# Sliding-window attention and a squared-ReLU FFN: first four chunks ahead of the weights, casting weight loads, an order written by hand, and crossbar transposes in the later blocks

## The chip, the cores and the metric

One core of a Trainium2 chip. The metric is the device time of one execution, in microseconds; the median of several runs counts. Engines are written PE (TensorE; PEld is its weight load), DVE (VectorE), ACT (ScalarE), POOL (GpSimd) and SP (SyncE, which issues transfers).

## What is computed

```python
# q, k, v: (8, 8, 576, 64) float32; moe_w_in: (512, 2048); moe_w_out: (2048, 512)
scores = (1/sqrt(D)) * q @ k.T          # per batch and head
mask = (rel >= 0) & (rel < 64)          # rel = query position - key position
attn = softmax(where(mask, scores, -1e9))
x = (attn @ v).transpose(0, 2, 1, 3).reshape(4608, 512)
h = maximum(x @ w_in, 0)
out = (h * h) @ w_out                   # (4608, 512) float32
```

## The kernel before

The 4608 tokens are cut into 36 chunks of 128 tokens and into 9 blocks of four chunks (512 tokens). Each query block of 64 tokens needs at most the 64 keys before it and its own 64. All matmuls are in float16.

For a chunk, `load` brings k, q and v as three tiles of 128 tokens x 8 heads x 64 (262 KB each, rows of 256 bytes) by SP's queue, and POOL casts them to float16 (L160 to L167). v is kept twice, in tiles shifted by 64 tokens (`v_ev`, `v_od`). Then four steps follow:

- `transposes` (L169): eight PE transposes bring k and q to head-dimension-major form in PSUM; DVE copies k to `kT` (L180), which also carries the 64 keys of the chunk before (L177), and ACT copies q to `qT` (L182).
- `scores` (L185): sixteen small matmuls, Exp on ACT (L199), and a minimum with a mask on DVE (L201).
- `values` (L204): sixteen small matmuls with a column of ones for the sum, then reciprocal and product on DVE (L215, L216), which give `x_sb`.
- `to_xT` (L221): four PE transposes of x and a DVE copy to `xT` (L226), one tile per block.

`ffn_up` takes a block: for each of 16 slices of d_ff, four matmuls of 512 columns (L250), a ReLU on ACT (L254) and a product on DVE (L255), which gives the square of the ReLU in `h2`. `ffn_up_chunk` does the same for one chunk, four slices at a time (L271 to L276), and is used for blocks 0 and 1. `ffn_out` does, for each 128 tokens of a block, 16 matmuls of 512 columns (L296), a copy by ACT that undoes the scale of the weights (L301) and an output transfer on SP (L303).

The weights come as float32 pieces of 262 KB through the pool `wst`: 16 of w_in, scaled by 100 and cast on DVE (L117), and 16 of w_out, cast on POOL (L130).

The program first asks for chunk 0, then all of w_in, then chunks 1 to 6, with `warm` matmuls between the steps of chunk 0; then chunk 7, w_out, and the ups of chunks 0 to 7 with the attention of the next chunks woven in. After that, the loop over g takes the output of block g-1, the up of block g, the attention of block g+1 and the loads of block g+2, mixed by `weave`. The framework's scheduler decides the final order on each engine: in the trace single matmuls of one group can stand between those of another.

Of the kernel before, what the change touches and what calls it, by code (L numbers as in the profile page):

```python
# [9 lines left out]
FP32 = mybir.dt.float32  # L10
# [3 lines left out]


def weave(*streams):

    keyed = []
    for s, (steps, lo, hi) in enumerate(streams):
        n = len(steps)  # L20
        for i, step in enumerate(steps):
            keyed.append((lo + (hi - lo) * (i + 0.5) / n, s, i, step))
    keyed.sort(key=lambda e: e[:3])
    return [e[3] for e in keyed]
# [3 lines left out]
def kernel(  # L28
# [17 lines left out]
    W_SCALE = 100.0  # L46
    OUT_SCALE = 1.0 / (W_SCALE * W_SCALE)
# [6 lines left out]
    wst = ctx.enter_context(tc.tile_pool(name="wst", bufs=4))  # L54
    stage = ctx.enter_context(tc.tile_pool(name="stage", bufs=15))
    st16 = ctx.enter_context(tc.tile_pool(name="st16", bufs=8))
    attw = ctx.enter_context(tc.tile_pool(name="attw", bufs=3))
# [8 lines left out]

    ident = const.tile([P, P], FP16, name="ident")
    make_identity(nc, ident[:])

    base = const.tile([P, 64], FP16, name="base")
    nc.gpsimd.memset(base[:], BIG)
    nc.gpsimd.affine_select(
        out=base[:], in_=base[:], compare_op=ALU.is_ge, fill=0.0, base=-1,
        pattern=[[-1, 64]], channel_multiplier=1,
    )
    nc.gpsimd.affine_select(  # L80
        out=base[:], in_=base[:], compare_op=ALU.is_ge, fill=0.0, base=64,
        pattern=[[1, 64]], channel_multiplier=-1,
    )
# [10 lines left out]
    mask_first = make_mask("mask_first", 0)  # L94
    mask_inner = make_mask("mask_inner", None)
    mask_second = make_mask("mask_second", 1)

    w_in_sb = const.tile([P, DMC, DFF], FP16, name="w_in_sb")
    w_out_sb = const.tile([P, FFC, DM], FP16, name="w_out_sb")

    NV = 8
    v_evs = [const.tile([P, H, 66], FP16, name=f"v_ev{i}") for i in range(NV)]
    v_ods = [const.tile([P, H, 66], FP16, name=f"v_od{i}") for i in range(NV)]
    for i in range(NV):
        nc.vector.memset(v_evs[i][:, :, 64:65], 1.0)
        nc.vector.memset(v_ods[i][:, :, 64:65], 1.0)
    nc.vector.memset(v_ods[0][0:64, :, 0:D], 0.0)

    def load_w_in():
        steps = []  # L110
        FQ = DFF // 4

        def one(quar, c):
            ws = wst.tile([P, FQ], FP32, name="ws", tag="ws")
            nc.sync.dma_start(out=ws[:], in_=moe_w_in[c * P:(c + 1) * P,  # L115
                                                      quar * FQ:(quar + 1) * FQ])
            nc.vector.tensor_scalar(  # L117
                out=w_in_sb[:, c, quar * FQ:(quar + 1) * FQ], in0=ws[:],
                scalar1=W_SCALE, scalar2=None, op0=ALU.mult)

        for quar in range(4):
            for c in range(DMC):
                steps.append(lambda quar=quar, c=c: one(quar, c))
        return steps

    def load_w_out():
        def one(f):
            ws = wst.tile([P, DM], FP32, name="ws2", tag="ws")
            nc.sync.dma_start(out=ws[:], in_=moe_w_out[f * P:(f + 1) * P, :])
            nc.gpsimd.tensor_copy(out=w_out_sb[:, f, :], in_=ws[:])  # L130

        return [lambda f=f: one(f) for f in range(FFC)]


    xTs = {}

    def xT_of(g):
        if g not in xTs:
            xTs[g] = xtp.tile([P, DMC, 512], FP16, name="xT", tag="xT")
        return xTs[g]  # L140

    q16s, k16s, qTs, kTs, pms, xs = {}, {}, {}, {}, {}, {}

    def load(i):

        sts = []
        for (src, nm) in ((k, "k"), (q, "q"), (v, "v")):
            st = stage.tile([P, H, D], FP32, name=f"{nm}_st", tag="st")
            b0, j0 = divmod(2 * i, NB)
            if j0 + 1 < NB:  # L150
                nc.sync.dma_start(  # L151
                    out=st[:], in_=src[b0, :, 64 * j0:64 * j0 + P, :].rearrange("h p d -> p h d"))
            else:
                nc.sync.dma_start(
                    out=st[0:64], in_=src[b0, :, 64 * j0:S, :].rearrange("h p d -> p h d"))
                nc.sync.dma_start(
                    out=st[64:P], in_=src[b0 + 1, :, 0:64, :].rearrange("h p d -> p h d"))
            sts.append(st)
        k16s[i] = st16.tile([P, H * D], FP16, name="k16", tag="k16")
        nc.gpsimd.tensor_copy(out=k16s[i][:], in_=sts[0][:].rearrange("p h d -> p (h d)"))  # L160
        q16s[i] = st16.tile([P, H * D], FP16, name="q16", tag="q16")
        nc.gpsimd.tensor_copy(out=q16s[i][:], in_=sts[1][:].rearrange("p h d -> p (h d)"))
        v_ev, v_od, v_next = v_evs[i % NV], v_ods[i % NV], v_ods[(i + 1) % NV]
        nc.gpsimd.tensor_copy(out=v_ev[:, :, 0:D], in_=sts[2][:])
        nc.gpsimd.tensor_copy(out=v_od[64:P, :, 0:D], in_=v_ev[0:64, :, 0:D])
        if i + 1 < NCK:
            nc.gpsimd.tensor_copy(out=v_next[0:64, :, 0:D], in_=v_ev[64:P, :, 0:D])  # L167
# [201 lines left out]
```

The softmax here doesn't subtract the row's maximum and nothing guards it: scores larger than these inputs give would overflow.

## Time and profile before

| | |
|---|---|
| median of 3 runs | 347.73 us (347.43 to 350.61) |
| span of the profiled execution, its own time | 345.9 us |
| PE busy | 324.3 us (94%), 3146 matmuls |
| DVE, ACT, POOL busy | 207.9, 163.8, 121.5 us |
| read from HBM, written | 36.70 MB, 9.44 MB |
| k, q, v tile of 262 KB | 3.9 to 4.1 us from issue to landing |
| output tile of 262 KB | 2.2 us from issue to landing |

The median of the runs is 1.8 us above the profiled span. In the profile, the busy rows cut the span in 40 slices of 8.6 us and give the busy share of each in tenths; a row of a timeline has its start, its duration, the engine, the line and the tiles. Matmuls overlap in the records, so what one costs is read from the distance of starts, not from its duration.

### The profile page before, as it was taken

To read this page: it belongs to the slowest core of one execution; us is meant where nothing else is said; L and a number is where in the kernel's file an instruction comes from. 1 tells how busy PE (TensorE), PEld (TensorE's weight loads), DVE (VectorE), ACT (ScalarE), POOL (GpSimd) and SP (SyncE) were. 2 spreads that over 40 slices of the span, in tenths; PEclk is the share of its full clock that TensorE was granted. 3 is DMA by queue.
4 is the path that set the end of the run, shared out by engine and by line. 5 is a ranking of instruction groups with operands and counts; after the bars stand their busy time and mean duration, and the time that the engine had idled before them with its cause. 6 is when DMAs were issued, how large, how long until landed. Compare 5 with 4: busy or idle time off the path is not lost.

```text
span 345.9 us, 7917 instructions
## 1 busy us (share of the span) xinstructions
PE 324.3 (94%) x3146; PEld 178.2 (52%) x3146; DVE 207.9 (60%) x506; ACT 163.8 (47%) x289; POOL 121.5 (35%) x204
## 2 busy tenths in 40 slices
PE   1957888999999999999999999999999999999995
PEld 0346787875555555445545554455445544544442
DVE  2656988852666776676776657665675566544400
ACT  1123457544535646643664466436544654444411
POOL 4009895497753333316566544530000000000000
PEclk9996999999999999999999999999999999999998
DMA  7799987899972455546877757730011000000021
GB/s 200 249 252 239 234 247 252 207 230 228 243 172 61 93 121 123 121 124 155 212 185 182 170 135 184 185 87 27 23 45 36 30 32 32 30 30 32 35 88 62
DMA packets 122341, 46.65 MB, mean 135 GB/s; under 512 B 113600, under 2 KB 113600, under 8 KB 122304
## 3 DMA queue, kind: packets, MB, share of 16 engines
q1 hardware_dynamic: 122304, 46.15, 51.7%
q8 instruction: 24, 0.39, 0.5%
q14 instruction: 13, 0.11, 0.1%
HBM read 36.70 MB, written 9.44 MB: 133 GB/s over the span
## 4 chain that ended last, share of the span: by engine, by line
PE 83%; DVE 7%; DMA 5%; ACT 2%; SPq 1%; issue 1%; ACTq 0%
PE ops L296 37%; PE hps L250 28%; DMA ws<-in_moe_w_in_dram 5%; PE qkT_ps L173 4%; PE av L211 4%; PE xt_ps L224 2%; DVE h_397 L276 1%; DVE h_1087 L276 1%; DVE xT L226 1%; DVE w_in_sb L117 1%; PE hps_639 L271 1%; SPq L151 1%; SPq L115 0%; PE hps_1088 L271 0%; PE hps_1537 L271 0%
## 5 line engine op out<-in xcount | busy, mean ns | idle before, releaser
L250 PE MATMUL hps<-xT,w_in_sb 128*128 128x512 f16 x448 | 115.2, 379 | 0.0
L254 ACT ACTIVATE hrelu<-hps 128x512 f32<-128x512 f32 x112 | 66.8, 598 | 91.6 <-PE hps L250 90.9
L250 PEld LDWEIGHTS <-w_in_sb 128*128 128x128 f16 x448 | 43.7, 98 | 52.6 <-issue 0.3
L271 PEld LDWEIGHTS <-w_in_sb 128*128 128x128 f16 x512 | 31.2, 99 | 8.2 <-issue 3.9
L301 ACT ACTIVATE osb<-ops 128x512 f32<-128x512 f32 x36 | 21.6, 600 | 29.1 <-PE ops L296 28.9
L182 ACT ACTIVATE qT<-qkT_ps 128x512 f16<-128x512 f16 x36 | 21.5, 596 | 22.6 <-DVE kT L180 22.3
L216 DVE TENSOR_TENSOR x_sb<-av,rden 128x256 f16<-128x256 f32 x72 | 27.5, 415 | 0.1
L180 DVE COPY kT<-qkT_ps 128x512 f16<-128x512 f16 x36 | 15.2, 421 | 18.0 <-PE qkT_ps L173 17.8
L226 DVE COPY xT<-xt_ps 128x512 f16<-128x512 f16 x36 | 15.1, 420 | 12.7 <-PE xt_ps L224 12.7
L215 DVE RECIPROCAL rden<-av 128x4 f32<-128x4 f32 x72 | 11.4, 178 | 17.1 <-PE av L211 17.1
L255 DVE SCALAR_TENSOR_TENSOR h_5222<-hps,hrelu 128x512 f16<-128x512 f32 x16 | 11.1, 691 | 16.6 <-ACT hrelu L254 16.6
L296 PE MATMUL ops<-w_out_sb,h_1087 128*128 128x512 f16 x64 | 17.5, 380 | 0.0
L191 PEld LDWEIGHTS <-kT 64*128 64x128 f16 x576 | 11.0, 95 | 12.2 <-issue 9.6
L296 PE MATMUL ops<-w_out_sb,h_3120 128*128 128x512 f16 x64 | 16.5, 380 | 0.0
L296 PE MATMUL ops<-w_out_sb,h_2579 128*128 128x512 f16 x64 | 16.5, 380 | 0.0
L296 PE MATMUL ops<-w_out_sb,h_4199 128*128 128x512 f16 x64 | 16.5, 380 | 0.0
L296 PE MATMUL ops<-w_out_sb,h_3658 128*128 128x512 f16 x64 | 16.5, 380 | 0.0
L296 PE MATMUL ops<-w_out_sb,h_2041 128*128 128x512 f16 x64 | 16.5, 380 | 0.0
L296 PE MATMUL ops<-w_out_sb,h_4736 128*128 128x512 f16 x64 | 16.4, 379 | 0.0
L296 PE MATMUL ops<-w_out_sb,h_397 128*128 128x512 f16 x64 | 15.3, 380 | 0.0
L224 PE MATMUL xt_ps<-ident,x_sb 128*128 128x128 f16 x144 | 15.1, 222 | 0.1
L255 DVE SCALAR_TENSOR_TENSOR h_4736<-hps,hrelu 128x512 f16<-128x512 f32 x16 | 11.0, 689 | 6.8 <-ACT hrelu L254 6.4
(837 smaller groups left out, 611.1 us busy)
## 6 DMA issues: line engine op xcount, KB each, us to landing
out_dram<-osb SPq DMA_DIRECT2D x36, 256.0 KB, 2.2
k_st<-in_k_dram SPq DMA_DIRECT2D x32, 256.0 KB, 3.9
q_st<-in_q_dram SPq DMA_DIRECT2D x32, 256.0 KB, 4.0
v_st<-in_v_dram SPq DMA_DIRECT2D x32, 256.0 KB, 4.1
ws<-in_moe_w_in_dram SPq DMA_DIRECT2D x16, 256.0 KB, 4.2
k_st<-in_k_dram SPq DMA_DIRECT2D x8, 128.0 KB, 3.2
q_st<-in_q_dram SPq DMA_DIRECT2D x8, 128.0 KB, 3.0
v_st<-in_v_dram SPq DMA_DIRECT2D x8, 128.0 KB, 3.2
```

The lines of the kernel that those rows point to most:

```text
L173: nc.tensor.transpose(out=ps[:, s, hp, :], in_=src[i][:, hp * P:(hp + 1) * P], identity=ident[:])
L180: nc.vector.tensor_copy(out=kT[:, :, 64:192], in_=ps[:, 0])
L182: nc.scalar.activation(out=qT[:], in_=ps[:, 1], func=AF.Copy, scale=1.0)
L216: nc.vector.tensor_tensor(out=x_sb[:, 4 * half:4 * half + 4, :], in0=av[:, :, 0:D], in1=rden[:].to_broadcast([P, 4, D]), op=ALU.mult)
L224: nc.tensor.transpose(out=xt[:, c, :], in_=xs[i][:, 2 * c:2 * c + 2, :], identity=ident[:])
L226: nc.vector.tensor_copy(out=xT_of(i // 4)[:, :, (i % 4) * P:(i % 4 + 1) * P], in_=xt[:])
L250: nc.tensor.matmul(hps[:], w_in_sb[:, c, f * P:(f + 1) * P], xT_of(g)[:, c, :], start=(c == 0), stop=(c == DMC - 1))
L254: nc.scalar.activation(out=hrelu[:], in_=hps[:], func=AF.Relu)
L255: nc.vector.scalar_tensor_tensor(out=h2s[g][:, f, :], in0=hps[:], scalar=0.0, in1=hrelu[:], op0=ALU.max, op1=ALU.mult)
L271: nc.tensor.matmul(hps[:, f, :], w_in_sb[:, c, (4 * fq + f) * P:(4 * fq + f + 1) * P], xT_of(g)[:, c, t0:t0 + P], start=(c == 0), stop=(c ...
L296: nc.tensor.matmul(hold["ps"][:], h2s[g][:, f, ts * P:(ts + 1) * P], w_out_sb[:, f, :], start=(f == 0), stop=(f == FFC - 1))
L301: nc.scalar.activation(out=osb[:], in_=hold["ps"][:], func=AF.Copy, scale=OUT_SCALE)
```

## The change

- Order at the start: chunks 0 to 3 are asked for first (q of chunk 0 by ACT's queue), then w_in in four quarters of 1 MB, then chunks 4 and 5 with w_out's quarters behind chunk 5's k and v casts. Ups of chunks 0 to 5 stand ahead of the output of block 0; the ups of chunks 6 and 7 and the attention of chunks 6 to 11 are mixed with it.
- The weights are cast in the transfer, which POOL issues. The pool `wst`, the DVE scaling and the POOL casts are gone. The scale moves to the ReLU (1e4).
- The order on PE, ACT, DVE, POOL and SP is pinned to the order in which the program writes the instructions.
- k and q of four chunks share a tile (`k16`, `q16`, `kT`, `qT`), and the keys across a block's border lie in a small tile `kB`. From block 4 on, `transposes_xbar` transposes k and q of a block by two transfers of SP (0.5 MB each) in place of the 64 PE transposes, and `boundary` fills `kB`.
- From block 3 on, `to_xT_xbar` transposes x of two chunks by one transfer of SP (0.26 MB).
- An Exp on one element at the start loads ACT's table; `warm` multiplies zeros and is called for 19 matmuls, not 26.

```diff
-    W_SCALE = 100.0
-    OUT_SCALE = 1.0 / (W_SCALE * W_SCALE)
+    H_SCALE = 1.0e4
+    OUT_SCALE = 1.0 / H_SCALE
-    wst = ctx.enter_context(tc.tile_pool(name="wst", bufs=4))
-    st16 = ctx.enter_context(tc.tile_pool(name="st16", bufs=8))
-    attw = ctx.enter_context(tc.tile_pool(name="attw", bufs=3))
+    kqp = ctx.enter_context(tc.tile_pool(name="kqp", bufs=2))
+    ktp = ctx.enter_context(tc.tile_pool(name="ktp", bufs=2))
+    attw = ctx.enter_context(tc.tile_pool(name="attw", bufs=4))
...
+    def load_w_in(quar):
+        nc.gpsimd.dma_start(
+            out=w_in_q[quar][:],
+            in_=moe_w_in[:, quar * FQ:(quar + 1) * FQ].rearrange("(c p) n -> p c n", p=P))
...
+    def transposes_xbar(g):
+        for key, dst in (("k", kT_of(g)), ("q", qT_of(g))):
+            nc.sync.dma_start_transpose(
+                out=dst[:].rearrange("p a (c t) -> p (a c) t", t=P),
+                in_=kqs[key, g][:].rearrange("p a c t -> p (a c t)"))
+
+    def boundary(g):
+        kB = kBs["b", g]
+        nc.vector.tensor_copy(out=kB[:, :, 0:64], in_=kTs["k", g - 1][:, :, 448:512])
+        nc.vector.tensor_copy(out=kB[:, :, 64:P], in_=kTs["k", g][:, :, 0:64])
...
+    def to_xT_xbar(i):
+        nc.sync.dma_start_transpose(
+            out=xT_of(i // 4)[:, i % 4 // 2].rearrange("p c (s t) -> p (c s) t", t=P),
+            in_=xs[i // 2][:].rearrange("p c s t -> p (c s t)"))
...
+    ctx.enter_context(tc.manual_schedule(engines={E.PE, E.Activation, E.DVE, E.Pool, E.SP}))
...
+    T, S, V, X, U = transposes, scores, values, to_xT, up_chunk
+    T(0), warm(3)
+    cast_chunk(1)
+    S(0), warm(3), T(1), warm(1)
+    cast_chunk(2)
+    V(0), S(1), warm(2), X(0), T(2), warm(1)
+    cast_kq("k", 3, sts[3][0], nc.gpsimd.tensor_copy)
+    for quar in range(3):
+        load_w_in(quar)
+    cast_kq("q", 3, sts[3][1], nc.scalar.copy)
+    cast_v(3, sts[3][2])
+    sts[4] = [load(x, 4) for x in (k, q, v)]
+    cast_kq("k", 4, sts[4][0], nc.gpsimd.tensor_copy)
+    load_w_in(3)
...
+    load_w_out(2)
+    load_w_out(3)
+    V(1), S(2), X(1), warm(1), T(3), V(2), S(3), U(0, 0), X(2), U(1, 0), U(2, 0), V(3)
+    load_chunk(6)
+    U(0, 1), U(1, 1), X(3), U(2, 1), U(0, 2), U(1, 2), U(2, 2), U(3, 0), U(3, 1), T(4)
+    load_chunk(7)
+    U(3, 2), U(0, 3), S(4), U(1, 3), U(2, 3), U(3, 3), V(4), T(5), X(4), S(5)
...
+    pairs = [(ts, fq) for a in (0, 2) for fq in range(4) for ts in (a, a + 1)]
+    steps = [((n + 0.5) / 16, out_proj, 0, ts, fq) for n, (ts, fq) in enumerate(pairs)]
+    for i in range(6, 12):
+        t = 0.17 + 0.115 * (i - 6)
+        steps += [(t, T, i), (t + 0.06, S, i), (t + 0.15, V, i), (t + 0.21, X, i)]
...
+    for g in range(2, NTB + 1):
+        G = g + 1
+        steps = [((n + 0.5) / 16, out_proj, g - 1, n // 4, n % 4) for n in range(16)]
+        if g < NTB:
+            steps += [((f + 0.8) / 16, up, g, f) for f in range(FFC)]
+        if G < NTB:
+            if G >= KQ_XBAR:
+                steps += [(0.02, boundary, G), (0.05, S, 4 * G)]
+            for j in range(4):
+                i, t = 4 * G + j, 0.18 * j
+                if G < KQ_XBAR:
+                    steps += [(t, T, i), (t + 0.07, S, i)]
+                steps.append((t + 0.17, V, i))
+                if G >= KQ_XBAR and j < 3:
+                    steps.append((t + 0.17, S, i + 1))
+                if G < X_XBAR:
+                    steps.append((t + 0.25, X, i))
+                elif j % 2:
+                    steps.append((t + 0.17, to_xT_xbar, i))
+        if g + 2 < NTB:
+            steps += [(0.03 + 0.17 * j, load_chunk, 4 * g + 8 + j) for j in range(4)]
+            if g + 2 >= KQ_XBAR:
+                steps.append((0.93, transposes_xbar, g + 2))
+        run(steps)
```

`run` calls the steps in the order of their first number, their place in the loop from 0 to 1. T, S, V and X are the four attention steps of a chunk, U is `up_chunk`.

## The prediction

> **What bounds the kernel now.** I read the busy slices first, then a table of windows cut where the program changes stage, then the timeline of TensorE inside one steady block, then the chain of waits of the first 75 us.
>
> ```profile
> PE   1957888999999999999999999999999999999995
> PEclk9996999999999999999999999999999999999998
> DMA  7799987899972455546877757730011000000021
> ```
>
> TensorE is full from slice 9 on (about 75 us). The DMA row is full in the first ten slices and never again. So there are two kernels in one: a start held by transfers, then a long part held by TensorE.
>
> ```profile
> 0.00:75.00 75.00, 57.78 (x894) 45.34 (x895) 52.23 (x142) 31.97 (x56) 43.04 (x78) 0.95 0.89 235
> 198.50:232.50 34.00, 34.00 (x307) 17.03 (x305) 21.95 (x52) 18.00 (x33) 16.00 (x26) 1.00 0.60 144
> 300.10:327.70 27.60, 27.60 (x129) 12.54 (x128) 11.06 (x16) 11.94 (x20) 0.00 (x0) 1.00 0.10 39
> 327.70:345.90 18.20, 14.02 (x65) 6.13 (x63) 0.69 (x1) 2.98 (x5) 0.00 (x0) 0.94 0.19 72
> ```
>
> Columns: window, length, busy time (count) of PE, PEld, DVE, ACT, POOL, clock, DMA share, GB/s. A steady block with attention lasts 34.0 us (that of 164.5 to 198.5 as well), all TensorE, while DVE has 12 us of slack and ACT 16. The block without attention (8) lasts 27.6. Attention therefore costs 6.4 us of TensorE in each block. What it consists of:
>
> ```profile
> 228.17 0.39 PE L224 MATMUL xt_ps<-ident,x_sb 128*128 128x128 f16 x4
> 228.39 1.03 PE L296 MATMUL ops<-w_out_sb,h_3120 128*128 128x512 f16 x4
> 229.25 1.03 PE L250 MATMUL hps<-xT,w_in_sb 128*128 128x512 f16 x4
> ...
> 232.07 0.39 PE L173 MATMUL qkT_ps<-ident,k_3718 128*128 128x128 f16 x4
> 232.29 0.39 PE L173 MATMUL qkT_ps<-ident,q_3720 128*128 128x128 f16 x4
> 232.51 1.03 PE L296 MATMUL ops<-w_out_sb,h_3658 128*128 128x512 f16 x4
> ```
>
> Only differences of starts count, since records overlap. x of one chunk: 228.39 - 228.17 = 0.22 us. k and q: 232.51 - 232.07 = 0.44. Four wide matmuls: 229.25 - 228.39 = 0.86, so 0.216 each, and 128 of them are the 27.6. Scores and values are the rest: 6.4/4 - 0.66 = 0.94 per chunk.
>
> ```profile
> 4.12 5.49 DMA ws<-in_moe_w_in_dram
> 10.09 4.25 DMA ws<-in_moe_w_in_dram
> 14.81 3.77 DMA ws<-in_moe_w_in_dram
> 19.72 5.40 DMA ws<-in_moe_w_in_dram
> ```
>
> These four pieces of the chain are w_in, which goes ahead of chunks 1 to 6. The first 19 us of the chain are w_in, and then TensorE has w_in but waits for chunks, one at a time, until 42 us. How fast the chunks come is on SyncE's timeline:
>
> ```profile
> 25.91 1.00 SPq L151 DMA_DIRECT2D k_st<-in_k_dram  x1
> ...
> 41.58 0.93 SPq L151 DMA_DIRECT2D v_st<-in_v_dram  x1
> 42.60 0.80 SPq L129 DMA_DIRECT2D ws_398<-in_moe_w_out_dram  x1
> ```
>
> Fifteen tiles of 262 KB are issued from 25.91 to 42.60: 3.93 MB in 16.7 us, 235 GB/s, with the queue pushing back. That is also the mean of the first window, so 240 GB/s is my price for anything in the start.
>
> **What the Trainium skill says.** VectorE: DVE Perf Modes, "The three transpose paths", gives 1309 ns for a 128x128 transpose by the crossbar and 390 ns by TensorE; here a TensorE transpose costs 0.055 us in a stream, far under the page, so I do not trust its other number as a rate either. DMA: Bandwidth & Descriptors, "Latency and other measured facts", gives 261 GB/s for crossbar transposes with a non-contiguous middle dimension, about 350 to 400 otherwise. No transfer in this trace is a transpose, so neither is confirmed. The same page, "Queues, rings and completion order", says that each DMA engine takes turns between queues packet by packet. The profile has 113600 packets under 512 B (k, q, v rows of 256 B), and weight rows are 2 KB: a second queue with large packets should win most of the engines' time. No two busy queues are in this trace to show it.
>
> **The change part by part.**
>
> (1) k and q transposes leave TensorE for blocks 4 to 8, x transposes for blocks 3 to 8: 160 and 96 fewer matmuls (L173 288 to 128, L224 144 to 48). The attention of block G lies in the loop of block G-1. Loop 2 loses 4 x 0.22 = 0.9 us; loops 3 to 7 lose 4 x 0.66 = 2.6 each, 13.2 in all. All of it is on TensorE, which is full, so it counts in full: -14.1. With them go copies (L180, L226 on DVE, 0.42 each, L182 on ACT, 0.6), which are worth nothing there: both engines have slack.
>
> (2) In their place SyncE issues two transposes of 0.5 MB (k, q) and two of 0.26 MB (x) in a loop. In program order on SyncE, k and q stand behind the loads of the loop, behind the output of its third row block (step 0.72) and behind x's second transpose (0.71). The loop is now 34.0 - 2.6 = 31.4 us, so they are issued at about 0.76 of it, 23.9 us. The first scores that read them stand at 0.05 of the next loop, 33.0 us: 9.1 us for both. At 261 GB/s they take 2.0 us each and, with the 2.2 us to landing that an output of half this size shows, both have ended after about 6: no stall. x is issued at 0.71 and read at 1.05, 10 us, no stall. Lower bound of this cost: 0. Upper bound: 16 blocks one after the other at the page's 1.309 us, 21 us for each transpose, 42 for both, 33 of stall in each of five loops. I take 0, because a transfer spread over 16 engines should not go block by block; the upper end goes to a rival. Queued behind the two transposes are an output and the next loop's loads; with 5.6 MB a loop (3.1 loads, 1.0 outputs, 1.5 transposes) at 240 GB/s the queue is busy 23 of 31.4 us, so these survive.
>
> (3) The start. Four chunks are loaded first (3.1 MB, 13 us at 240 GB/s plus 2.9 to the first landing), then w_in as four 1 MB casting transfers from GpSimd's queue, issued once k of chunk 3 is cast, at about 15 us. Its packets are eight times as long as those of k, q, v, so I give it three quarters of the engines: 4.4 us a quarter, landing at about 20, 25, 29 and 33. TensorE does the attention of chunks 0 to 3 meanwhile and then takes the quarters as they come, three to five chunks on each; 24 pieces of 0.89 us (16 starts, 19.41 to 20.30 in the trace) and 1.6 per chunk bring it to chunk 5's end at about 50.
>
> Then comes the mixed stage: output of block 0 (13.8), up of chunks 6 and 7 (7.1), attention of chunks 6 to 11 (6 x 1.6 = 9.6): 30 us of TensorE, so 80 at best. By then 12 chunks and both weights are needed: 9.4 + 8.4 = 17.8 MB, 74 us at 240 GB/s, 77 with the first landing. k and q of chunk 11 are due at three quarters of the stage; if they land at 75 and are cast 1.3 later, 7 us remain: 83. I take 82. The same point of the kernel before: out of block 2 begins at 130.4, one block earlier is 96.4. Gain 14.4, bounds 8 (DMA at 220 GB/s, w_in late) and 20 (TensorE bound alone).
>
> (4) Priced at nothing: the w_in scaling on DVE (16 x 0.43) and the w_out casts on GpSimd (16 x 0.61) that disappear; against them stand eight descriptor jobs on GpSimd, unknown, taken at 1 us each (0.3 to 3), with the casts of v 3, k 4 and on queued behind them. At 3 us each the casts of chunk 4 and 5 still precede 34 us, when they are read. Boundary copies of 64 keys: 0.2 us of DVE, twice a block. The order written by hand on all engines: in the steady block outputs and ups alternate as before, scores stand 5 us ahead of their values, so I see no new wait there; in the mixed stage DVE has 6 x 2.9 (copies, masks, divisions of a chunk) + 8 x 0.69 = 23 us of work in 30, close, and that is in the bounds of (3).
>
> **Sum.** 82 + loop 2 (33.1) + five loops (157.0) + block 8's up (27.6) + the end (18.2) = 317.9 us of span, against 345.9. The median of the runs is 1.8 above the profiled span; with that, 319.7: I say 320.
>
> **Rivals.**
> *The crossbar is slow (ends slower).* One mechanism: first scores of each block wait for qT at the head of loops 3 to 7, and TensorE executes in order, so the whole loop stands. Slack is 9.1 us for the two. The gain elsewhere, 28 us, is used up at 5.6 us of stall in each of five loops, so from (9.1 + 5.6)/2 = 7.3 us per transpose, 72 GB/s. At 10 us each the stall is 10.9 x 5 = 54: 374 us. For it: the page's 1309 ns for one small block, and the late place on SyncE. Against: the bandwidths on the other page, and a DMA row at 1 to 5 tenths over this part.
> *The start gives nothing.* w_in shares the engines with k, q, v evenly, or the casting transfers move less than 240 GB/s; the order by hand then makes each late piece stop all of TensorE, where the trace before shows pieces of another group slipped between transposes. Start ends at 96 as now; only (1) remains: 334. For it: DMA is at 0.89 in this window already, and total bytes are the same. Against: 17 us of TensorE idle in the window.
> *DVE binds the mixed stage*: its 23 us, stretched by half through waits taken in order, fill 35 instead of 30: 325, inside the range. For it: 8.95 of 10 us are busy at 60 to 70 us now. Against: from block 2 on it has a third of its time free.
>
> **How the numbers follow.** Forecast (309 to 331) 0.60; start gives nothing, or a crossbar stall of a few us (331 to 344) 0.16; slow crossbar 0.17; within 1% of before 0.04; better than 309 0.03. Range 309 to 344. About 1% is what a measurement here tells from no change: faster 0.79, same 0.04, slower 0.17.
>
> **What would show it.** Right: TensorE full from about 50 us, its blocks 3 to 7 at 31.4 us, start of the out matmuls of block 2 near 115, no wait of L193 for a transfer. Crossbar wrong: waits of L193 (or of the boundary copies) on DMA kT or qT at each loop's head. Start wrong: L268 waiting for w_in quarters, L163 for GpSimd's casts between 50 and 80. The forecast is wrong if a transpose of 0.5 MB takes over 5 us, or if the start ends after 90.

## The result: 336.0 us, and the profile after

The changed kernel takes 335.97 us (335.79 to 336.24) against 347.75 us of the kernel before on the same chip, a ratio of 0.964 [0.961, 0.968]. That is 11.8 us faster; 28 were forecast. The profiled execution has a span of 333.8 us, where the sum of the prediction gave 317.9.

The busy slices of the changed kernel's page, to be held against the three rows of the kernel before (a slice is 8.3 us now):

```profile
PE   6749968999899999999999999999999999999995
PEclk9787998999999999999999999999999999999999
DMA  9999999999449769968979796989599121200111
```

TensorE starts earlier than before, but the digits of its first eleven slices keep changing (4 in the third, 6 in the sixth, 8 in the eleventh), and the clock row has a 7 or an 8 in four of the first seven. DMA, which stood at 2 to 8 from slice 12 to 27 and nearly idle after it, now stands at 4 to 9 and stays busy to slice 31.

The windows of the changed kernel, cut at the first output matmul of blocks 0, 1 and 2 (first stage, mixed stage, loop 2), from block 3 to 4 (a loop with the crossbar) and from 7 to 8 (the loop without attention); columns as in the prediction (window, length, busy time of PE, PEld, DVE, ACT, POOL, clock, DMA share, GB/s; the DMA share is given as the view has it and can pass 1):

```profile
0.00:60.29 60.29, 45.34 (x667) 36.99 (x668) 35.21 (x100) 27.04 (x47) 30.60 (x55) 0.89 1.14 196
60.29:96.14 35.85, 32.51 (x467) 21.37 (x465) 24.39 (x61) 16.51 (x31) 23.85 (x38) 1.00 0.76 160
96.14:129.23 33.09, 32.83 (x284) 15.88 (x281) 19.55 (x44) 17.52 (x32) 12.85 (x20) 1.00 0.84 170
161.04:192.82 31.78, 31.09 (x257) 14.65 (x256) 19.25 (x42) 16.07 (x28) 12.60 (x20) 1.00 0.92 183
288.17:315.80 27.63, 27.63 (x130) 12.51 (x129) 11.06 (x16) 11.94 (x20) 0.00 (x0) 1.00 0.11 39
```

Against the prediction's sum: the start ends at 96.1 instead of 82 (+14.1), loop 2 takes 33.1 as said, the five loops with the crossbar 158.9 instead of 157.0 (+1.9), block 8 and the end 45.6 instead of 45.8. The whole gap of 15.9 us is therefore in two places, and nine tenths of it in the start. The start splits into a first stage, to the first output matmul (60.3 us, forecast 50), and the mixed stage (35.9 us, forecast 30, taken as 32 with its late loads).

What TensorE waits for, in the changed kernel (total, times, longest; the five largest):

```profile
PE xt_ps L232 <- DVE x_sb L222: 3.9, 8, 1.0
PE sc L193 <- DMA qT<-q: 3.5, 5, 0.7
PE hps L268 <- DMA w_in<-in_moe_w_in_dram: 3.3, 1, 3.3
PE sc L193 <- ACT qT L168: 2.4, 6, 0.7
PE hps L268 <- DVE h L250: 1.5, 4, 0.5
```

The second line is the crossbar: five loops, 0.7 us each, together the 3.5 us that the loops have above 31.1. The third is the weight, once. The others are small waits for answers of DVE and ACT, many places of half a microsecond. They are easily passed over, since none is large, but in the first stage they and the weight make up 14.8 us, and in the mixed stage 3.2. What stands behind them is seen on DVE's and ACT's own timelines. One turn of the mixed stage, DVE first, then ACT (start, duration, and in brackets the idle time before it and its releaser):

```profile
84.34 0.69 DVE L250 SCALAR_TENSOR_TENSOR h<-hps,hrelu 128x512 f16<-128x512 f32 x1 [1.15 <-ACT hrelu L249]
...
86.05 1.57 DVE L206 TENSOR_TENSOR pm<-pm,mask_inner 128x512 f16<-128x512 f16 x2
87.54 0.68 DVE L250 SCALAR_TENSOR_TENSOR h<-hps,hrelu 128x512 f16<-128x512 f32 x1
88.14 0.41 DVE L235 COPY xT<-xt_ps 128x512 f16<-128x512 f16 x1
88.47 0.41 DVE L167 COPY kT<-qkT_ps 128x512 f16<-128x512 f16 x1
90.03 0.69 DVE L250 SCALAR_TENSOR_TENSOR h<-hps,hrelu 128x512 f16<-128x512 f32 x1 [1.15 <-ACT hrelu L249]
```

```profile
88.91 0.60 ACT L168 ACTIVATE qT<-qkT_ps 128x512 f16<-128x512 f16 x1 [2.92 <-DVE kT L167]
89.41 0.59 ACT L249 ACTIVATE hrelu<-hps 128x512 f32<-128x512 f32 x1
```

DVE's product at 84.34 is followed by everything that the program wrote behind it, up to the copy of k at 88.47. ACT's copy of q waits 2.92 us for that copy, and the ReLU that DVE's next product needs is queued behind ACT's copy. Then DVE waits 1.15 us for the ReLU. Neither engine is busy all the time, and each is waiting for the other. This is called the ring below: product, copy of k, copy of q, ReLU, and the next product. The same product stands at 79.26, 84.34 and 90.03 us, a turn of 5.1 to 5.7 us. In the whole stage DVE is busy 24.4 of 35.9 us and ACT 16.5, and no row of busy shares says that they hold TensorE up.

The start's transfers. TensorE meets the first quarter of w_in (its timeline), and SyncE issues chunk loads beside the casting transfers (its timeline):

```profile
23.38 1.89 PE L268 MATMUL hps<-xT,w_in 128*128 128x128 f16 x16 [3.34 <-DMA w_in<-in_moe_w_in_dram]
```

```profile
22.50 6.41 SPq L81 DMA_DIRECT2D st<-in_q_dram  x1
...
40.93 9.14 SPq L81 DMA_DIRECT2D st<-in_v_dram  x1
```

The record of the sixteen matmuls at 23.38 lasts 1.89 us, and that of sixteen at 41.06, at clock 1.00, lasts 1.07: the first ones run at about half the clock. One issue of a 262 KB load holds SyncE for 6.4 and 9.1 us.

And the crossbar in a steady loop, on SyncE's timeline and on TensorE's:

```profile
156.56 1.89 SPq L174 DMA_TRANSPOSE kT<-k  x1
158.54 2.85 SPq L174 DMA_TRANSPOSE qT<-q  x1
```

```profile
163.62 0.20 PE L193 MATMUL sc<-qT,kB 64*128 64x64 f16 x2 [0.69 <-DMA qT<-q]
```

k's transpose is issued 27.3 us after the loop's begin (129.23), not 23.9, and the issue of q's ends 4.8 us later. Ahead of k's in SyncE's order stand x's second transpose, issued at 25.3 us of the loop where the prediction's place 0.71 is 22.3, and an output behind it. The transpose of q lands 0.7 us after the scores could have begun.

### The profile page after: what moved, and what is told of

Read it like the earlier page. It is cut to its first block, busy times and chain, and to the rows that moved or that the text cites. A ratio compares the mean times of both kernels' runs of the same rounds, so it can differ in the third digit from the quotient of the medians.

```text
span 333.8 us, 7260 instructions
## 1 busy us (share of the span) xinstructions
PE 307.7 (92%) x2883; PEld 166.2 (50%) x2883; DVE 186.0 (56%) x431; ACT 156.3 (47%) x274; POOL 116.9 (35%) x191
## 3 DMA queue, kind: packets, MB, share of 16 engines
q0 software_dynamic: 4224, 4.19, 7.8%
## 4 chain that ended last, share of the span: by engine, by line
PE 58%; DMA 14%; DVE 11%; SPq 7%; ACT 4%; POOL 2%; issue 2%; ACTq 0%; POOLq 0%
PE ops L285 26%; PE hps L256 20%; DMA qT<-q 7%; PE hps L268 7%; DMA st<-in_v_dram 5%; SPq L81 4%; DVE h L250 4%; ACT hrelu L249 3%; PE sc L193 3%; PE av L217 3%; DVE pm L206 2%; DVE x_sb L222 2%; SPq L174 2%; DMA w_in<-in_moe_w_in_dram 2%; POOL v_ev L104 1%
## 5 line engine op out<-in xcount | busy, mean ns | idle before, releaser
L250 DVE SCALAR_TENSOR_TENSOR h<-hps,hrelu 128x512 f16<-128x512 f32 x144 | 99.1, 690 | 109.7 <-ACT hrelu L249 109.3
L285 PE MATMUL ops<-w_out,h 128*128 128x512 f16 x576 | 145.5, 379 | 0.6 <-DVE h L250 0.6
L256 PE MATMUL hps<-xT,w_in 128*128 128x512 f16 x448 | 115.1, 379 | 0.0
L285 PEld LDWEIGHTS <-h 128*128 128x128 f16 x576 | 53.8, 98 | 61.4 <-issue 0.8
L256 PEld LDWEIGHTS <-w_in 128*128 128x128 f16 x448 | 42.8, 98 | 50.1
L202 ACT ACTIVATE pm<-sc 128x512 f16<-128x512 f32 x72 | 39.1, 596 | 15.1 <-PE sc L193 14.5
L268 PE MATMUL hps<-xT,w_in 128*128 128x128 f16 x512 | 35.8, 233 | 6.1 <-DMA w_in<-in_moe_w_in_dram 3.3
L104 POOL CAST v_ev<-st 128x512 f16<-128x512 f32 x36 | 23.6, 656 | 42.5 <-DMA st<-in_v_dram 36.9
L268 PEld LDWEIGHTS <-w_in 128*128 128x128 f16 x512 | 33.2, 106 | 8.0 <-issue 3.7
L206 DVE TENSOR_TENSOR pm<-pm,mask_inner 128x512 f16<-128x512 f16 x56 | 29.0, 539 | 8.4 <-ACT pm L202 7.9
L107 POOL COPY v_od<-v_ev 64x512 f16<-64x512 f16 x35 | 22.7, 650 | 2.0
L105 POOL COPY v_od<-v_ev 64x512 f16<-64x512 f16 x36 | 22.5, 625 | 2.3
## 6 DMA issues: line engine op xcount, KB each, us to landing
w_in<-in_moe_w_in_dram POOLq DMA_DIRECT2D x4, 512.0 KB, 10.2
```

The source lines that it names most:

```text
L104: nc.gpsimd.tensor_copy(out=v_ev[:, :, 0:D], in_=st[:])
L202: nc.scalar.activation(out=pm[:], in_=sc[hh][:], func=AF.Exp, scale=1.0 / float(D) ** 0.5)
L206: nc.vector.tensor_tensor(out=pm[:], in0=pm[:], in1=mask, op=ALU.min)
L250: nc.vector.scalar_tensor_tensor(out=out, in0=hps, scalar=0.0, in1=hrelu, op0=ALU.max, op1=ALU.mult)
L256: nc.tensor.matmul(hps[:], w_in_q[f // 4][:, c, f % 4 * P:(f % 4 + 1) * P], xT_of(g)[:, :, c, :], start=(c == 0), stop=(c == DMC - 1))
L268: nc.tensor.matmul(hps[:, f, :], w_in_q[fq][:, c, f * P:(f + 1) * P], xT_of(g)[:, i % 4 // 2, c, a:a + P], start=(c == 0), stop=(c == DMC ...
```

## The experiments

A number like "60.3 + 35.9" below is the time of the first output matmul of block 0 (end of the first stage) and from there to that of block 1 (the mixed stage), read from the timelines of TensorE; loops means the mean distance of the same matmul from block to block between 2 and 7 (loops 3 to 7). Two theories stood at the beginning. Theory A: the order fixed by hand puts steps too close behind the answers of DVE and ACT that they need. Theory B: the transfers bound the start.

**Without the crossbar.**

```diff
-    KQ_XBAR = 4
-    X_XBAR = 3
+    KQ_XBAR = 99
+    X_XBAR = 99
```

> The changed kernel with its crossbar transposes taken back (k, q, x by TensorE in all blocks). If the steady blocks were priced rightly (14.1 us saved on TensorE, less five waits of 0.7 us for qT that the trace shows), it is 10.6 slower than the changed kernel: 346.6 us, and the new start is then worth about 1 us against the kernel before. If the gain of 11.8 came from the start instead, it stays within 3 us of 336.

Measured: 352.17 us, 1.011 [1.008, 1.014] of the kernel before. The crossbar is thus worth 16.2 us here, more than either expectation had it, and the rest of the change is a loss of 4 us. Loops take 34.9 us, 0.9 more than the kernel before with the same TensorE work, and 0.9 more than the same kernel without the fixed order (34.0, in the run with neither): the fixed order costs in the steady loops too.

**A quarter of the weights' bytes.** The casting transfers bring only the first quarter of each tile; the rest of the weights is filled with a constant by DVE and POOL.

```diff
-            out=w_in_q[quar][:],
-            in_=moe_w_in[:, quar * FQ:(quar + 1) * FQ].rearrange("(c p) n -> p c n", p=P))
+            out=w_in_q[quar][:, 0:1],
+            in_=moe_w_in[0:P, quar * FQ:(quar + 1) * FQ].rearrange("(c p) n -> p c n", p=P))
...
+        nc.vector.memset(w_in_q[quar][:, 1:4], 0.01)
```

> Leaves out three quarters of both weights' transfers (constants stand in their place), so 6.3 MB less crosses in the first 80 us; all orders stay. Theory A (each step of TensorE stands too close behind the DVE and ACT work that it needs, in the pinned order; the data is there): only the wait of 3.3 us for the first quarter of w_in and perhaps 2 us of half clock go: 331 us (329 to 333). Theory B (transfers bind the start, as the forecast's rival said): the start ends near 80 instead of 96, 320 to 324 us.

Measured: 334.99 us, 0.959 [0.955, 0.963]; 60.7 + 34.8. With 6.3 MB less to read the mixed stage is 1 us shorter. So theory B falls for the mixed stage. The time lies in neither theory's range (329 to 333, 320 to 324). For the first stage the run is not clean: its waits show TensorE standing 5.5 us for the first k behind DVE's new fills, where the changed kernel stands 0.4. Without these 5.1 us the stage would have ended at some 55.6 us (an estimate), about 5 earlier than in the changed kernel, which waits 3.3 us for the first weight. So in the first stage the transfers may be worth up to that much.

**Nothing pinned.**

```diff
-    ctx.enter_context(tc.manual_schedule(engines={E.PE, E.Activation, E.DVE, E.Pool, E.SP}))
```

> The changed kernel without the line that pins the engines' order, so that the framework's scheduler places instructions. Theory A: in the start it slips other work between a step and its answer, 325 to 332 us, if the later blocks do not lose by it. Theory B: within 2 us of 336.

Measured: 326.03 us, 0.935 [0.933, 0.938], ten microseconds less than the changed kernel. The windows of this kernel, mixed stage and one loop:

```profile
58.11:89.68 31.57, 31.05 (x459) 20.87 (x457) 22.86 (x60) 16.18 (x30) 23.82 (x38) 1.00 0.88 179
153.99:185.01 31.02, 31.02 (x257) 14.62 (x256) 19.29 (x42) 15.96 (x28) 16.82 (x28) 1.00 1.04 213
```

The mixed stage falls to 31.6 and TensorE is busy in 31.1 of it, with the same matmuls, loads and casts; the loops take 31.1 in the mean (31.0 from loop 4 on), and no score waits for a transpose in them. What the prediction said of both, 32 and 31.4, holds here. The first stage still takes 58.1: the scheduler's order has its own waits (4.8 us once for qT from ACT, 3.6 us for q from POOL). The ring is here too: the products that stood at 79.26, 84.34 and 90.03 us stand at 73.86, 78.66 and 83.63, turns of 4.8 and 5.0 us. So of the 4.3 us that the mixed stage loses by the fixed order, the two turns shown hold 1.0, and 3.2 are lost before the first of these products.

**The first stage respaced by hand, and the mixed stage too.** Up-projections of a quarter are moved so that a step stands farther behind its source; in the mixed stage scores and values are set apart.

```diff
-    U(0, 1), U(1, 1), X(3), U(2, 1), U(0, 2), U(1, 2), U(2, 2), U(3, 0), U(3, 1), T(4)
+    U(0, 1), U(1, 1), X(3), U(0, 2), U(2, 1), T(4), U(1, 2), U(3, 1), S(4), U(2, 2), U(0, 3)
...
-        steps += [(t, T, i), (t + 0.06, S, i), (t + 0.15, V, i), (t + 0.21, X, i)]
+        steps += [(t, T, i), (t + 0.07, S, i), (t + 0.19, V, i), (t + 0.30, X, i)]
```

> The same work, the same transfers in the same order, but in the start and in the mixed stage values, x transposes and ups of a chunk stand further apart in the pinned order, and neighbouring ups use different PSUM pools. Theory A: 7.5 us of waits before 60 us and about 6 between 60 and 96 go, less what the arrival of chunks 7 to 11 then holds back: 324 to 329 us. Theory B: within 2 us of 336.

Measured: 331.65 us, 0.951 [0.947, 0.954]; 54.6 + 37.0. The first stage wins 5.7 us from order alone. The mixed stage loses 1.2: two of its scores now wait together 3.1 us for qT. My second spacing was a miss, and the time stays above theory A's range (324 to 329).

**In whose queue?** Three more kernels pin fewer engines; the engines named stay in the changed kernel's order to the instruction.

```diff
-    ctx.enter_context(tc.manual_schedule(engines={E.PE, E.Activation, E.DVE, E.Pool, E.SP}))
+    ctx.enter_context(tc.manual_schedule(engines={E.PE, E.Pool, E.SP}))
```

> Pins PE, POOL and SP only; DVE and ACT are ordered by the scheduler, and PE's own order is that of the changed kernel to the instruction. It asks in whose queue the 10 us sit that the pinning costs. Theory A1 (PE's order: a step stands on PE before the answer it needs can be there, whatever DVE and ACT do in the meantime): 334 to 338 us, with the out-projection of block 1 beginning at 94 to 98 us as in the changed kernel. Theory A2 (the order on DVE and ACT: a mask minimum or a copy queued behind one that PE does not need yet): 326 to 329 us, with that matmul at about 89 us.

```diff
+    ctx.enter_context(tc.manual_schedule(engines={E.PE}))
```

> PE alone pinned, in the changed kernel's order to the instruction; DVE, ACT, POOL and SP are ordered by the scheduler. Theory A4 (PE's order costs what is left, 3.3 us, wherever the casts and loads stand): 328 to 330 us, as with DVE and ACT free. Theory A5 (the rest sits in POOL and SP, whose casts and loads come in the order of the program): 325.5 to 327 us, as with nothing pinned.

```diff
+    ctx.enter_context(tc.manual_schedule(engines={E.Activation, E.DVE, E.Pool, E.SP}))
```

> PE alone free, ordered by the scheduler; DVE, ACT, POOL and SP in the changed kernel's order to the instruction. Theory A1 (a PE that may put other work ahead of what is not ready hides the ring of DVE and ACT): 326 to 329 us. Theory A2 (the ring of DVE and ACT sets the pace, PE cannot outrun it): 333 to 337 us, the mixed stage 34 to 36 us.

| pinned | time, us | ratio to before | start, us | loops, us |
|---|---|---|---|---|
| all five | 335.97 | 0.964 [0.961, 0.968] | 60.3 + 35.9 | 31.8 |
| PE, POOL, SP | 329.32 | 0.946 [0.944, 0.948] | 58.3 + 34.1 | 31.3 |
| PE | 329.38 | 0.946 [0.942, 0.950] | 60.2 + 33.9 | 31.0 |
| DVE, ACT, POOL, SP | 334.03 | 0.961 [0.957, 0.965] | 63.5 + 34.0 | 31.6 |
| none | 326.03 | 0.935 [0.933, 0.938] | 58.1 + 31.6 | 31.1 |

Freeing DVE and ACT wins 6.6 us. Freeing POOL and SP on top shows nothing in the time: the start is longer by 1.7 and the loops are shorter. Freeing TensorE alone shows about 2, and the two intervals overlap. So two thirds of the loss come back with DVE and ACT free, and a TensorE free to do other work first cannot outrun their queues. The last 3 us come only when TensorE is free as well. My first expectation for the DVE and ACT run put the seat wholly on one side or the other; it is neither.

Two readings of the traces narrow this. With DVE and ACT free, ACT's order differs from the changed kernel's by three exchanged pairs, and DVE's at 161 of 431 places: what comes back is almost all won in DVE's queue. And the 6.6 us do not lie mainly in the mixed stage: it gives 1.7 of them, the first stage 2.0 and the loops from loop 2 on 2.8.

**The copy of q first.** Both copies read one PSUM tile, and the program makes the second wait for the first. Two lines of `transposes` change places:

```diff
-        nc.vector.tensor_copy(out=k_dst, in_=k_src)
         nc.scalar.activation(out=q_dst, in_=q_src, func=AF.Copy, scale=1.0)
+        nc.vector.tensor_copy(out=k_dst, in_=k_src)
```

> The changed kernel with two lines swapped: of the two copies of a chunk's transposes out of one PSUM tile, ACT's copy of q comes first and DVE's copy of k second. The order of instructions on every engine stays the same; what turns round is the wait between the two. As changed, ACT's copy waits for DVE's, and in the mixed stage ACT stands 13.8 us so, with the ReLUs that DVE and PE need queued behind it (the ring: DVE product, divisions, masks, product, copy of k, then ACT copy of q, ReLU, then DVE product again, 5.4 us a turn). Theory A3 (this ring is what stretches the mixed stage from 30.8 to 35.9 us): mixed stage 31 to 33.5 us, first stage shorter by 0.5 to 2 us, 331 to 334 us. Rival (the ring closes elsewhere, since PE reaches the next up-projection only when DVE has come through its queue): mixed stage 35 to 36 us, 335 to 337 us.

Measured: 332.26 us, 0.954 [0.950, 0.958], 3.7 us less than the changed kernel; 57.5 + 35.0. The groups of this kernel from 58 to 93 us (busy, mean ns, idle before and releaser) show the wait turned round:

```profile
L167 ACT ACTIVATE qT<-qkT_ps 128x512 f16<-128x512 f16 x7 | 4.2, 597 | 4.9 <-PE qkT_ps L163 4.8
L168 DVE COPY kT<-qkT_ps 128x512 f16<-128x512 f16 x6 | 2.5, 419 | 3.6 <-ACT qT L167 3.6
```

ACT's wait for DVE's copy (13.8 us in the changed kernel's mixed stage) is gone, and the first stage is 2.8 us shorter. The time falls in the interval of theory A3, but the mixed stage won only 0.9, where I expected 2 to 5: there the rival was right. DVE now waits for ACT, and the mixed stage is hardly shorter. This member of the ring is not what holds most of the stage's loss.

**The loop's first scores later.** The boundary copies go from 0.02 to 0.08 of the loop, the first scores from 0.05 to 0.12.

```diff
-                steps += [(0.02, boundary, G), (0.05, S, 4 * G)]
+                steps += [(0.08, boundary, G), (0.12, S, 4 * G)]
```

> Steady loops only: the copies of the shared rows of a block's keys (boundary) go from place 0.02 to 0.08 of the loop, the first scores of the block from 0.05 to 0.12, so that the block's queries and keys have some 2 us more to land. Theory A (the 0.7 us wait of the scores for qT in each of the five loops with the crossbar is a wait on a late transfer and nothing else): loops 31.1 us instead of 31.8, the start as in the changed kernel, 332 to 333 us. Rival (the loop's order is bound elsewhere and the wait moves on to the values and to xT): 335 to 337 us.

Measured: 337.48 us, 0.968 [0.965, 0.971], no gain. The waits of this kernel's TensorE:

```profile
PE av L217 <- DVE pm L206: 5.8, 13, 0.6
```

The scores' wait for the transpose of q is gone from the list. In its place the values wait for their masks, 13 times in all (3 times and 1.1 us before the edit), ten of them and 4.4 us in the five loops: by the program's places the first values, at 0.17, now stand 0.05 of a loop behind their scores instead of 0.12. The loops take 32.2. I was wrong to think the wait free to remove: in a fixed order a step that is moved back stands nearer to the one behind it.

**Neither crossbar nor pinning.** Both edits, the constants at 99 and no pinned order.

> No crossbar transposes and no pinned order: only the new start, the casting weight loads and the new buffers are left of the change. If the pinning (10 us) and the crossbar (-16 us) add up: 326 + 16 = 342 us, that is 6 us under the kernel before, all of it in the start (out-projection of block 1 at about 89 us), with loops of 34 us as before. If the crossbar's saving was 16 only because the pinned order left PE's transposes waiting, then the crossbar is worth the 2.6 us a loop that its PE work measures, 326 + 14 = 340 us or less. If the new start is worth nothing without the crossbar: 347 us.

Measured: 342.23 us, 0.983 [0.980, 0.986]; 58.7 + 31.3, loops 34.0. With the other three corners: the crossbar is worth 16.2 us pinned (352.17 - 335.97) and 16.2 free (342.23 - 326.03); pinning costs 9.9 and 9.9. The two effects add up, as the first expectation had it, and the new start alone is worth 6.

**Only the first stage pinned.** The respaced first stage stays pinned, the scheduler orders the rest (`first` is the same manual order, left after chunk 5's up-projection).

```diff
+    first.__exit__(None, None, None)
     load_chunk(9)
     load_chunk(10)
```

> Order pinned up to chunk 5's up-projection alone, with the respaced first stage of the earlier run (its first out-projection at 54.6 us), and the scheduler orders everything after it. Theory A, in which the two stages lose separately: 54.6 + 30.8 us of mixed stage + 229 us from there on as in the kernel without pinning, that is 322 to 324 us. Rival (the mixed stage is then bound by the chunks 6 and 7, whose loads and casts on POOL are no earlier than before): the first out-projection at 54.6 us, but the second still at 88 to 91 us, 326 to 329 us.

Measured: 323.94 us, 0.932 [0.926, 0.939]; 54.4 + 31.8. The two stages lose separately, as theory A has it. One later loop takes 33.0 instead of 31.0: a boundary copy on DVE waits for kT and TensorE for the product behind it, 1.8 us.

**w_in's first quarter earlier**, in that kernel: issued at 12.4 us instead of 16.7.

```diff
     cast_chunk(1)
+    load_w_in(0)
```

> The previous kernel (first stage pinned and respaced, the scheduler after it), with the transfer of w_in's first quarter issued behind the casts of chunk 1 instead of behind those of chunk 2 and the first of chunk 3: about 12.5 us instead of 16.7 us. There PE waits 4.1 us for that quarter (20.0 to 24.1 us) and then runs at half clock for some 6 us. Theory A (late transfer, and the half clock is its echo): the wait is nearly gone, the clock holds, the first out-projection at 49 to 51 us instead of 54.4, 319 to 321 us. Rival (DMA: the earlier weight takes the place of the loads of chunks 2 and 3, whose casts and scores come as much later): the first out-projection stays at 53 to 55 us, 323 to 325 us.

Measured: 51.4 + 31.9, so the start ends at 83.3 us. The first stage won its 3 us. The time did not come down with it in most executions: three took 326.4 to 328.5 us and one 321.1, too far apart for a ratio. In the profiled one, of 326.4 us, loop 2 takes 38.1 us; its chain of waits (start, duration, what):

```profile
104.46 6.43 DMA kT<-k
...
110.92 0.23 DVE kB L181
...
111.28 0.61 DVE h L250
...
111.93 1.02 PE hps L256 x4
```

The order on TensorE, DVE, ACT and SyncE is that of the kernel without this edit, and there too the transpose of k for block 4 lands at 110.7 us; the boundary copy on DVE waits 1.0 us for it. Now the loop has begun 3 us earlier and the transpose, issued 1.9 us earlier, takes 6.4 us and lands at 110.9. The copy waits 4.7 us, a product of the up-projection stands behind the copy, TensorE stands 3.5 us, and the clock from 111 to 121 us is 0.83. This is the prediction's rival of the slow crossbar, in one place; that one execution took 321.1 us says that it need not come each time.

**The clock held**, in the kernel with the first stage pinned: ten idle matmuls before the first up-projection.

```diff
-    V(1), S(2), X(1), warm(1), T(3), V(2), S(3), U(0, 0), X(2), U(1, 0), V(3), U(2, 0)
+    V(1), S(2), X(1), warm(1), T(3), V(2), S(3), warm(10), U(0, 0), X(2), U(1, 0), V(3), U(2, 0)
```

> The kernel with the first stage pinned and respaced, plus ten idle matmuls (2.2 us) into a spare PSUM tile ahead of the first up-projection, inside the 4.1 us in which PE waits for w_in; nothing else. It measures the clock's share alone. If the half clock from 21.8 us on follows from PE's pause: it is shorter or gone, the matmuls of the first up-projections take 0.86 us for sixteen at once instead of 1.9, the first out-projection at 52 to 53.5 us instead of 54.4, 322 to 323 us. If the half clock has another cause or what follows waits for DVE and ACT anyway: 54.4 us and 324 us as without.

Measured: 324.14 us, 0.932 [0.926, 0.937], as without; first stage 53.8 instead of 54.4. TensorE's timeline:

```profile
20.38 4.33 PE L277 MATMUL warm<-zeros 128*128 128x512 f16 x10
24.54 1.06 PE L268 MATMUL hps<-xT,w_in 128*128 128x128 f16 x16
```

The first up-projections are at full speed (1.06 us for sixteen instead of 1.89), but the ten idle ones took 4.33 us, twice what I counted, at a clock of 0.53: the half clock was paid in them. The first stage is 0.6 us shorter; why the clock falls is not settled. The run is clean for the first stage only. The ten matmuls changed the scheduler's order behind the pinned part (DVE's at 29 of 431 places, with the boundary copy now ahead of a product and two masks), and in the profiled execution, 326.6 us and the longest of the four, loop 2 takes 37.7 us:

```profile
PE hps L256 <- DVE h L250: 2.9, 1, 2.9
```

It is the same wait as in the run before, in a kernel whose w_in is not early.

**The boundary copy off DVE**, on the kernel with w_in early. TensorE's order is the same to the instruction.

```diff
-        nc.vector.tensor_copy(out=kB[:, :, 0:64], in_=kTs["k", g - 1][:, :, 448:512])
-        nc.vector.tensor_copy(out=kB[:, :, 64:P], in_=kTs["k", g][:, :, 0:64])
+        nc.gpsimd.tensor_copy(out=kB[:, :, 0:64], in_=kTs["k", g - 1][:, :, 448:512])
+        nc.gpsimd.tensor_copy(out=kB[:, :, 64:P], in_=kTs["k", g][:, :, 0:64])
```

> The previous kernel (first stage pinned and respaced, first quarter of w_in early, the scheduler after it) with one edit: the two copies of a block's shared key rows (boundary) are done by POOL instead of DVE; PE's order is the same to the instruction. There the copy stood on DVE ahead of two products of the up-projection and waited for the crossbar's kT of block 4, which landed at 110.9 us; PE stood 3.5 us and ran at half clock after it, and loop 2 took 38.1 us. Theory A (a wait for the crossbar is paid only by what is queued behind it, and on DVE that is PE's food): loop 2 takes 33.2 us as in the kernel before it, 318 to 321 us. Rival (the crossbar's lateness is itself the bound: the scores need kT at that time wherever the copy stands, or the casts behind the copy on POOL make the next crossbar later still): loop 2 stays at 36 to 38 us, 324 to 328 us.

Measured: 320.01 us, 0.919 [0.916, 0.922], the best of all; its six executions lie between 318.8 and 321.3. Its windows:

```profile
0.00:51.89 51.89, 39.72 (x676) 32.45 (x676) 34.92 (x101) 27.18 (x48) 26.43 (x48) 1.00 1.18 196
51.89:83.11 31.22, 31.12 (x459) 20.87 (x457) 22.68 (x60) 16.24 (x30) 22.50 (x35) 1.00 1.01 208
83.11:116.21 33.10, 32.87 (x283) 15.77 (x281) 20.19 (x45) 17.51 (x32) 19.92 (x33) 1.00 1.13 217
```

Loop 2 is back at 33.1 us and the start still ends at 83.1. The copy waits on POOL now, 2.5 us for a transpose that lands no earlier (111.2), and no step that TensorE needs soon is queued behind it there. The one short execution of the run with w_in early, 321.1 us, is nearly as fast: what the edit takes away is the late loop of the other three. Only one later loop is long (32.4 instead of 31.0), with a wait of 1.2 us for a transposed x.

## Why the prediction was wrong, and where it was right

*What bounds it.* Right: the steady blocks are TensorE's, and the start is where time lies idle. "A start held by transfers" was half right for the kernel before and carried too far for the new one.

*Step (1), transposes off TensorE, -14.1.* Right in kind, a little small: 16.2 us with and without pinning. A loop loses 3.0 us when the order is free (34.0 to 31.0), where I counted 2.6. (The counts of this step are right; k and q of a block are 32 PE transposes, not the 64 given under the change.)

*Step (2), the crossbar at nothing.* Right but for 3.5 us. Two terms were mis-sized. The transposes are issued 3.4 us later than worked out. And issue takes SyncE 1.9 and 2.9 us for the pair, so q's is not on its way with k's but behind it: 6.9 us for both, not 6. The slack of 9.1 us became a wait of 0.7. This too belongs to the fixed order: with nothing pinned the two are issued at 11.8 and 15.6 us of a loop (that of 153.99 to 185.01), and no score waits for them. From the changed kernel's list of queues (packets, MB) and of transfers (KB written by each, median us to landing):

```profile
q0 software_dynamic: 4224, 4.19, 7.8%
...
w_in<-in_moe_w_in_dram POOLq DMA_DIRECT2D x4, 512.0 KB, 10.2
...
kT<-k SPq DMA_TRANSPOSE x5, 4.6
qT<-q SPq DMA_TRANSPOSE x5, 4.6
```

4.6 us is close to the estimate of 2.0 + 2.2; the 2.0 came from the bandwidth in the Trainium skill (DMA: Bandwidth & Descriptors, "Latency and other measured facts"), the 2.2 from the outputs of the trace before. The rival's 1.3 us for each of 16 small blocks, 21 us, is far off.

*Step (3), "I take 82", with the sentence of step (4), "The order written by hand on all engines: ... so I see no new wait there".* This is where it failed. The start ended at 96.1. I priced it as a bound of transfers and of TensorE's work, and took the order for something that costs nothing. It costs 10 us: with all of it undone the start is 6.5 us shorter, loops 2 and 3 by 0.2 to 0.4 each, and the loops 4 to 7 by 0.7 to 0.8 each. The parts of the 14.1 us, each from one run on top of the other: the order inside the first stage 5.9 (60.3 to 54.4), the order in the mixed stage 4.0 (35.9 to 31.8), w_in's late first quarter 3.0 (54.4 to 51.4). Sum 12.9, and the start ends at 83.3. The quarter was in my text with 4.4 us to land; it took 6.6 from issue to landing, and the median of the four is 10.2. The 4.4 was wrong by my own premise: 1.05 MB take 4.4 us at the whole 240 GB/s and 5.8 at the three quarters that I gave them. Nor are the packets eight times as long: the profile counts 4224 packets for 4.19 MB in the queue of the casting transfers (q0 in the list above), about 1 KB each, four times a row of k, q or v. The descriptor jobs on POOL, taken at 1 us, took 0.74 to 0.87. Of the signs that I named, "the start ends after 90" and the wait of L268 for w_in came.

*The rivals.* The time fell where "the start gives nothing" put it (334). That it is so near is partly luck, for the cause is not the first that I gave. Less weight moved the mixed stage by 1 us only, so bytes do not bind it. What I mentioned last, that an order by hand makes each late piece stop all, cost the start 6.5 us. The third rival, DVE binding the mixed stage through "waits taken in order", said 35 us for that stage; it took 35.9. I put this rival inside the range and priced it on top of 320 as 5 us. The number is right, the mechanism in part: freeing DVE and ACT wins 1.7 of the 4.3 us in this stage, and 2.0 and 2.8 us in the first stage and in the loops, where the rival did not look. The profile before held a hint that I read and put aside: from 60 to 70 us DVE was busy 8.95 of 10. The slow crossbar came true in small in the changed kernel (five waits of 0.7) and, after the first stage had been repaired, at one place for 2.9 and 3.5 us of TensorE.

*With the order mended.* The last kernel of the experiments, with a fixed order in the respaced first stage alone and w_in's first quarter early, takes the 320 us of the forecast. Its start ends at 83.1 us, where I took 82, and its loops take 31.3 in the mean: the sum of work and transfers was about right, and what failed was the price of the order and of one late transfer.

*What stays open.* That the fixed order costs 10 us is shown with and without the crossbar, and that most of it goes through DVE's queue by the five ways of pinning. The ring is seen in the timelines, but it turns in the free order too, and which steps must move to free the mixed stage isn't shown: the copy of q gave 0.9 of 4.3 us, my respacing made it worse. Nor is it settled why the granted clock halves at 22 us. The program alone doesn't fix it: the two kernels with w_in early have the same order on TensorE, and up to the first output matmul (51.4 and 51.9 us) the profiled execution of one has a mean clock of 0.97, that of the other 1.00.

## What to carry to other kernels

Fixing the order on all engines is not free: price it as one more resource, by following one value round the engines (product, copy, ReLU, product) and asking what is queued between on each. Engines that are far from full can make each other wait, and no busy share shows it. Where a wait for a transfer can't be excluded, put it on an engine behind which nothing of the bound one is queued. And a repair must be followed to the first loop after it: when a start is shortened, or the scheduler's order shifts, the next transfer on the line can become the late one.

## What the runs showed of the hardware

- A transfer by the crossbar of 0.5 MB takes 4.6 us from issue to landing in the median of the changed kernel (4.4 to 4.9) and up to 6.8 us in the kernels with a freer order. Issuing it keeps SyncE for 1.9 to 2.9 us there, more than a plain load of a steady loop (0.4 to 1.4 us).
- Two queues on the same engines: while the casting transfers of 1 MB ran, single issues of 256-byte-row loads took 6.4 and 9.1 us. The Trainium skill has each DMA engine take turns between its queues, packet by packet (DMA: Bandwidth & Descriptors, "Queues, rings and completion order"); that a load is held up beside a second queue fits this. The large share for the weights that the prediction drew from it does not show: 10.2 us, not 4.4. No run here measures how the turns fall.
- At half clock the record of sixteen 128-column matmuls lasts 1.89 us, at full clock 1.06. Ten idle matmuls that were to bridge a pause ran at half clock too.
